# Token mixing of a fused retention and MLP kernel: one 2x2 block product with seven quarter products for eight, and the first loads issued on two queues

## The chip, the cores and the metric

The kernel runs on one core of one Trainium2 chip. The metric is the device time of one execution in microseconds (us), the median over runs. TensorE is called PE here, VectorE DVE, ScalarE ACT, GpSimd POOL, and SyncE SP.

## The reference

Inputs are float32, with batch B = 2, H = 8 heads, S = 768 tokens, head size D = 64, model size DM = 512 and inner size DFF = 1024. Three layers follow each other:

```python
# 1 retention, per head, gamma of the head
state = gamma * state + k[t] v[t]^T ;  y[t] = q[t] state / sqrt(D)
# 2 channel mixing (x is y, x_prev the token before)
xk, xr = mu_k*x + (1-mu_k)*x_prev, mu_r*x + (1-mu_r)*x_prev
x = sigmoid(xr @ w_r) * (relu(xk @ w_k)**2 @ w_v)
# 3 gated MLP with token mixing
h = gelu_tanh(x @ w_in) ;  u, v = h[..., :512], h[..., 512:]
v_n = (v - mean(v)) / sqrt(var(v) + 1e-6) * g_ln
v_s = einsum('ts,bsd->btd', w_sg, v_n) + b_sg[None, :, None]
return x + (u * v_s) @ w_out
```

The change concerns the line of `v_s`, a product of a 768x768 matrix with a 768x512 matrix for each of two batches, and what stands behind it.

## The kernel before

Every dense product is computed as three passes over pairs of rounded halves: an operand is split into a high part (a cast to fp32r) and a low part (the rest), and `passes` (L333) lists high x high, high x low, low x high. `dense` (L319) issues the matmuls of one output tile in three thirds, one for each pass, each a step of its own. `split` (L314) makes the parts: a cast on ACT or DVE and a subtraction on DVE.

The order of all work is made by a planner, the class `Plan`. Each step names its engine, a cost, and the buffers that it reads, writes and needs anew; `Plan.order` (L88) plays the steps through with these costs and writes down the order, which is then each engine's queue, executed strictly in order. A step for "DVE ACT" goes to whichever is free first. SP issues loads and stores, "ADD" stands for accumulating transfers that POOL issues. Buffers come from pools with fixed numbers of slots (`slots`, L208): `p4` (18 of 128 x 2 x 512 words), `t` (13 of 128 x 512), `raw` (3 landing buffers), `ps` (the 8 banks into which PE writes), and single slots aA, aB, bA, bB and cA for split weights.

The program in order: retention in chunks of 128 tokens (`loads` L353, `scores`, `decay`, `state`, `inter`, `intra`, `tokens`), twelve (batch, chunk) pairs, whose `qk` and `kv` tiles of 512 KB are all issued by SP; ten matmuls of zeros (`warm_mm`, L392) run while the first load is under way. Channel mixing follows: `k_tile` (L564), `r_tile` (L568), and the product with `w_v`, in which two blocks of 256 tokens already go by seven quarter products (L580 to L732), with weight sums that accumulating transfers make (`sum_weights`, L603).

Layer 3 works on three blocks of 256 tokens, n = 0, 1, 2. For each n and batch, `c1` (L799) computes the v half, token on partition, with its normalisation on DVE, and splits it into the tiles `vh`; `wsg` (L866) loads and splits one sixth of `w_sg`; `c2` (L854) computes the u half. `c3(g, m)` (L875) is token mixing: for g = 0 and 1 it makes the first 512 tokens of batch g and 128 features in 18 matmuls of 512 columns; for g = 2 the last 256 tokens of both batches in 2 x 18 matmuls of 256 columns. Behind each tile, DVE multiplies by the gain and adds the bias (L888), multiplies by u (L896) and splits the result `gt`. `c4(g)` (L901) multiplies by `w_out`, 12 matmuls of 512 columns for each of 4 m, adds x on DVE (L910) and stores. The calls stand in L917 to L934:

```python
for g in range(B):
    for m in range(KD):
        c3(g, m)
c4(0)
for m in range(KD):
    c3(B, m)
for g in range(1, B + 1):
    c4(g)
```

Of the kernel before, what the change touches and what calls it, by code (L numbers as in the profile page):

```python
# [35 lines left out]
WARM_UP = 10  # L36
EARLY = 5
# [3 lines left out]
T_SLOTS = 13  # L41
# [17 lines left out]
class Plan:  # L59
# [28 lines left out]
    def order(self):  # L88
# [16 lines left out]
        engines = ("PE", "DVE", "ACT", "POOL", "SP", "ADD")  # L105
        idle = {e: BEGIN for e in engines}
        queue = {e: [] for e in engines}
        seq, events, link = [], [(BEGIN, -1, e) for e in engines], 0.0
        started = [False] * n
# [30 lines left out]
        def start(i, t, eng):  # L140
            nonlocal link
# [13 lines left out]
            if eng in ("SP", "ADD"):  # L155
                busy = t + (ISSUE if eng == "SP" else ADD_ISSUE)
                late = link > t + DMA_LEAD + 1.0
                link = max(t + DMA_LEAD, link) + cost / DMA_RATE
                done = link + (DMA_TAIL if late else 0.8)
            else:  # L160
                busy = done = t + cost
# [43 lines left out]
def fused_kernel(ctx, tc, qk, kv, w_k, w_v, w_r, w_in, w_sg, w_out, consts, ydec, b_sg, out):  # L205
# [4 lines left out]
                        "t": {"rs": EARLY, "vs": 2, "cv": 2, "mix": 2, "rk": 2, "vt": 6, "t2": 4, "u": 6, "g": 2, "o": 2}},  # L210
# [142 lines left out]
    def loads(i, what):  # L353
# [38 lines left out]
    def warm_mm():  # L392
        for _ in range(WARM_UP):
            pe.matmul(out=T["warmps"], lhsT=T["warm"][:, :128], rhs=T["warm"], start=True, stop=True)
# [4 lines left out]
    plan.op("PE", 4.0, warm_mm, r=[("warm", 0)], w=[("warmps", 0)], new=[new_b("warm", "warmps")])  # L399
    loads(0, "q")  # L400
    plan.op("SP", .11, const, w=[("con", 0)])
# [110 lines left out]
    for c in range(NCH):  # L512
# [286 lines left out]
    def c1(n, b):  # L799
# [5 lines left out]
        for e in range(2):  # L805
# [6 lines left out]
                    r=[(ps, 0)], w=[(v, e)], new=[new("raw", "raw", v, (128, 2, DM))] if e == 0 else [])  # L812
# [20 lines left out]
        for e in range(2):  # L833
            o = ("vh", b, 2 * n + e)
# [3 lines left out]
            split(lambda e=e: T[v][:, e], o, 0, lambda o=o: T[o][:, 0], lambda o=o: T[o][:, 1], [(v, e)],  # L838
                  [new_p("vh", o)])
# [3 lines left out]
    def u_homes(n):  # L843
        if n == 0:
            return [(new_t("u", ("u", n, m)), ("u", n, m), lambda m=m: T["u", n, m]) for m in range(KD)]
        if n == 1:
            b = ("u", n, "p")
            return ([(new_t("u", ("u", n, m)), ("u", n, m), lambda m=m: T["u", n, m]) for m in range(2)] +
# [166 lines left out]
```

## Time and profile before

| | us |
|---|---|
| median of 3 runs | 357.09 (356.94 to 358.16) |
| the profiled execution's own time | 359.38 |
| its span, first to last instruction | 357.6 |
| PE busy in it | 347.6, 97% |
| DVE busy | 255.8, 72% |
| ACT busy | 159.7, 45% |
| POOL busy | 28.8, 8% |

The span of the profiled execution is the base of the sums; the 1.8 us between it and the execution's own time lie outside of the instructions. The rows that follow below the change are whole lines of the profile's page and of answers of the trace. In the groups, "xcount | busy, mean ns of one | idle before" follows the shapes; in the chain and the timeline, the start and the length come first.

### The profile page before, as it was taken

Reading aid. Unit: us, or ns where it says so; the run is one execution under the profiler, and the core shown is the slowest. Engines: PE = TensorE matmul, PEld = TensorE weight load, DVE = VectorE, ACT = ScalarE, POOL = GpSimd, SP = SyncE. Lnnn points to the kernel's source line nnn. Section 1 sums busy time; section 2 is a strip of 40 time slices with the busy share of each in tenths; the row PEclk is TensorE's granted clock in tenths of the full one; section 3 lists DMA queues with packets and bytes.
Section 4 is the critical chain, followed back from the end, with each engine's and each line's share of the span. In section 5 each row is a group of like instructions: output and inputs, shape, how many; then the busy total and the mean of one; then the engine's idle time right before and its main releaser. Section 6 shows DMA issues by size and latency. Waiting matters only on the chain.

```text
span 357.6 us, 5412 instructions
## 1 busy us (share of the span) xinstructions
PE 347.6 (97%) x2130; PEld 289.7 (81%) x2130; DVE 255.8 (72%) x501; ACT 159.7 (45%) x274; POOL 28.8 (8%) x29
## 2 busy tenths in 40 slices
PE   7988999999999999999999999999999999999995
PEld 4777788888888888888888888888888888899884
DVE  1778999898992664568699998999995656535431
ACT  1044669888972543345589659734542000000000
POOL 0453400000002122101100000000000000000000
PEclk9999999999999999999999999999999999999999
DMA  7999555135544669406354245121130000110122
GB/s 252 415 408 409 210 185 170 59 92 161 158 141 98 106 183 168 73 3 173 66 172 119 60 122 173 44 79 55 45 88 2 0 0 0 60 59 2 58 90 89
DMA packets 15689, 43.32 MB, mean 121 GB/s; under 512 B 1456, under 2 KB 3632, under 8 KB 15664
## 3 DMA queue, kind: packets, MB, share of 16 engines
q1 hardware_dynamic: 12944, 37.73, 30.9%
q0 software_dynamic: 2720, 5.24, 8.6%
q8 instruction: 17, 0.28, 0.3%
q14 instruction: 8, 0.07, 0.1%
HBM read 32.48 MB, written 3.15 MB: 100 GB/s over the span
## 4 chain that ended last, share of the span: by engine, by line
PE 88%; DMA 7%; DVE 3%; issue 1%; SPq 0%; ACT 0%; DVEq 0%; ACTq 0%
PE vp L327 26%; PE kp L327 18%; PE sp L327 14%; PE up L327 9%; PE rp L327 9%; PE op L327 7%; DMA chunk<-qk 3%; DMA chunk<-kv 2%; DMA out<-o 2%; PE y L489 2%; PE sc L416 1%; PE y L478 1%; DVE o L910 1%; DVE xo L316 1%; PE st L452 1%
## 5 line engine op out<-in xcount | busy, mean ns | idle before, releaser
L327 PE MATMUL kp<-xo,wk 128*128 128x512 f32 x288 | 66.2, 390 | 0.0
L327 PEld LDWEIGHTS kp<-xo,wk 128*128 128x128 f32 x288 | 53.9, 188 | 11.5 <-issue 0.3
L327 PE MATMUL sp<-wsg,vh 128*128 128x512 f32 (+1 forms) x288 | 50.2, 336 | 0.0
L327 PEld LDWEIGHTS sp<-wsg,vh 128*128 128x128 f32 x288 | 44.4, 190 | 5.7
L327 PE MATMUL vp<-k,wv 128*128 128x512 f32 x168 | 38.9, 389 | 0.0
L327 PEld LDWEIGHTS vp<-k,wv 128*128 128x128 f32 x168 | 31.5, 188 | 6.5
L327 PE MATMUL vp<-win,x2o 128*128 128x512 f32 x144 | 33.3, 389 | 0.0
L327 PE MATMUL up<-x2o,win 128*128 128x512 f32 x144 | 33.1, 389 | 0.0
L327 PE MATMUL rp<-xo,wr 128*128 128x512 f32 x144 | 33.1, 389 | 0.0
L327 PE MATMUL op<-gt,wout 128*128 128x512 f32 x144 | 33.0, 389 | 0.0
L327 PEld LDWEIGHTS rp<-xo,wr 128*128 128x128 f32 x144 | 27.0, 188 | 5.6
L327 PEld LDWEIGHTS vp<-win,x2o 128*128 128x128 f32 x144 | 27.0, 188 | 5.6
L327 PEld LDWEIGHTS up<-x2o,win 128*128 128x128 f32 x144 | 27.0, 188 | 5.6
L327 PEld LDWEIGHTS op<-gt,wout 128*128 128x128 f32 x144 | 27.0, 188 | 5.6
L888 DVE SCALAR_TENSOR_TENSOR g<-sp,con,bsg 128x512 f32<-128x512 f32 x12 | 9.0, 751 | 21.8 <-PE sp L327 21.8
L316 DVE TENSOR_TENSOR xo<-mix,xo 128x512 fp32r<-128x512 f32 x24 | 17.0, 735 | 8.9 <-ACT xo L249 8.8
L910 DVE TENSOR_TENSOR o<-op,x 128x256 f32<-128x256 f32 (+1 forms) x20 | 8.8, 474 | 19.8 <-PE op L327 13.8
L275 ACT ACTIVATE cv<-raw 128x512 f32<-128x512 f32 x32 | 21.5, 670 | 1.9 <-DMA raw<-w_in 0.7
L327 PE MATMUL vp<-k,ws 128*128 128x512 f32 x96 | 22.1, 389 | 0.0
L612 POOL DMA_DIRECT2D raw<-wv x10 | 12.1, 1211 | 116.9 <-DMA raw<-wv 86.4
L327 PEld LDWEIGHTS vp<-k,ws 128*128 128x128 f32 x96 | 18.0, 188 | 3.7
L290 DVE SCALAR_TENSOR_TENSOR cv<-cv,raw 128x512 int32<-128x512 int32 x28 | 19.8, 714 | 0.6 <-ACT raw L283 0.6
(104 smaller groups left out, 464.5 us busy)
## 6 DMA issues: line engine op xcount, KB each, us to landing
chunk<-qk SPq DMA_DIRECT2D x12, 512.0 KB, 10.1
chunk<-kv SPq DMA_DIRECT2D x12, 512.0 KB, 10.1
raw<-wv POOLq DMA_DIRECT2D x10, 512.0 KB, 5.1
raw<-w_k SPq DMA_DIRECT2D x8, 512.0 KB, 5.3
raw<-w_v SPq DMA_DIRECT2D x8, 512.0 KB, 3.6
raw<-w_in SPq DMA_DIRECT2D x8, 512.0 KB, 3.5
out<-o SPq DMA_DIRECT2D x12, 256.0 KB, 2.2
raw<-w_sg SPq DMA_DIRECT2D x6, 384.0 KB, 3.2
```

The lines of the kernel that those rows point to most:

```text
L275: plan.op("ACT", .68, lambda: act.activation(out=xf(), in_=word(1).bitcast(F32), func=ACTF.Prelu, scale=-F64_REBIAS * F64_SIGN, alpha=1.0 ...
L290: dve.scalar_tensor_tensor(out=xi(), in0=xi(), scalar=3, in1=word(0), op0=ALU.logical_shift_left, op1=ALU.bitwise_or)
L316: plan.op("DVE", .69, lambda: dve.tensor_tensor(out=lo(), in0=src(), in1=hi(), op=ALU.subtract), r=[*keep, (buf, ("hi", part))], w=[(buf, ...
L327: pe.matmul(out=T[ps][:, cols], lhsT=l(), rhs=r(), start=first and q == 0 and i == 0, stop=q == 2 and i == len(grp) - 1, skip_group_check= ...
L416: pe.matmul(out=T["sc", i, p][:, j * CH:(j + 1) * CH], lhsT=a[par[p], 1, j], rhs=a[par[p], 0, j], start=j == 0, stop=j == KD - 1, skip_gro ...
L452: pe.matmul(out=st[par[p], b, j], lhsT=T["kv", i][:, 0, h], rhs=T["vs", i][:, h], start=c == 0 and b == 0 and j == 0, stop=b == B - 1 and ...
L478: pe.matmul(out=y_at(i, j, p), lhsT=T["sbd", (c - 1) % 2][par[p], b, j], rhs=T["qk", i][par[p], 0, j], start=b == 0 and j < 2, stop=False, ...
L489: pe.matmul(out=y_at(i, j, p), lhsT=T["vs", i][:, 2 * j + p], rhs=T["pr", i % 4][:, p, j], start=c == 0 and b == 0 and j < 2, stop=b == B ...
L612: plan.op("ADD", .53, lambda t=t: pool.dma_start(out=T[raw], in_=block_view(*t), accum_op=ALU.add), r=[(b, ("hi" if not t[2] else "lo", p) ...
L888: dve.scalar_tensor_tensor(out=out_, in0=in_, scalar=T["vec"][:, 2, m:m + 1], in1=t.unsqueeze(1).to_broadcast([128, B, BW]) if last else t ...
L910: plan.op("DVE", .69 if g == B else .42, lambda n=n, ps=ps, o=o, m=m, part=part, of=of: dve.tensor_tensor(out=T[o][:, part], in0=T[ps][:, ...
```

## The change

**Token mixing.** The token axis is cut into halves of 384 output tokens, h = 0 and 1, the sum over tokens into even and odd chunks of 128, and the two batches are the two columns of a 2x2 block product. Seven products of (384 x 384) by (384 x 512 features) stand for eight. Each is 4 m x 9 matmuls of 384 columns, 252 in all, where 144 of 512 and 144 of 256 columns stood. Two of the seven add into the banks of an earlier one (`first=False`). The seven weight blocks are sums of one to four quarters of `w_sg`, made by a plain load and accumulating transfers (`sg_sum`: 7 loads and 7 transfers of POOL, 576 KB each), then split (`sg_split`). DVE makes sums of the normalised values (`g_terms`, and in `g_m4`), splits seven sets of three operands (`g_operand`), and combines the products (`stt` and the steps behind it).

**Around it.** `c4` works on (half, batch), 16 tiles of 12 matmuls of 384 columns where 12 of 512 stood, with stores of 192 KB. The normalised values live in `p4` and not in `raw`, `u` in `p4` and in a spare weight slot, and pool `t` has 12 slots. `out` is laid out with the whole token axis in a row.

**Start.** The first two `kv` loads are issued on ACT's queue, the constants go ahead of the first `qk` load on SP's, and three more matmuls of zeros stand behind the scores of chunk 0. The planner's model of loads has a second link for ACT's queue.

```diff
-T_SLOTS = 13
+T_SLOTS = 12
...
-            plan.op("SP", .525, lambda: sp.dma_start(out=T["kv", i], in_=kv[b, c]), r=hold, w=[(("kv", i), 0)],
+            plan.op("SP" if hold else "AQ", .525, lambda: (sp if hold else act).dma_start(out=T["kv", i], in_=kv[b, c]), r=hold, w=[(("kv", i), 0)],
...
+    plan.op("SP", .11, const, w=[("con", 0)])
     loads(0, "q")
-    plan.op("SP", .11, const, w=[("con", 0)])
...
+                if step is scores and i == 0:
+                    plan.op("PE", .65, lambda: warm_mm(FILL), r=[("warm", 0)], w=[("warmps", 0)],
+                            after=plan.writer[("sc", 0, 0), 0])
...
+    def sg_sum(name, terms):
+        raw = ("raw", name)
+        for i, (h, e) in enumerate(terms):
+            view = w_sg[:, e::2, h * HS:(h + 1) * HS]
+            if i == 0:
+                plan.op("SP", .59, lambda view=view: sp.dma_start(out=T[raw], in_=view), w=[(raw, 0)],
+                        new=[new("raw", "raw", raw, (128, NB, HS))], after=plan.writer[("kv", 1), 0])
+            else:
+                plan.op("ADD", .59, lambda view=view: pool.dma_start(out=T[raw], in_=view, accum_op=ALU.add), w=[(raw, 0)])
...
+    def g_product(kind, ps, m, name, weights, first=True):
+        wb, at = sg_at[weights]
+        dense("sp", ps, .1745, passes([
+            ((("gh", name, n), 0, lambda h, n=n: T["gh", name, n][:, h, m * 128:(m + 1) * 128]),
+             (wb, at, lambda h, n=n: T[wb][h][:, at, n])) for n in range(NB)]), first=first, cols=cut, more=True)
+
+    def stt(out, in0, m, op1, in1, r, w, new=()):
+        plan.op("DVE", .56, lambda: dve.scalar_tensor_tensor(out=out(), in0=in0(), scalar=GAIN(m), in1=in1(),
+                                                            op0=ALU.mult, op1=op1), r=[("con", 0), *r], w=[w], new=new)
...
+    def g_n6():
+        for n in range(NB):
+            g_operand("t2", n, g2_at(n))
+        for m in range(KD):
+            ps, v = ("gb", m), ("gv", m)
+            g_product("gb", ps, m, "t2", "g2")
+            stt(half(v), half(ps), m, ALU.subtract, half(v), [(ps, 0)], (v, 0))
+            buf, part, view = v0(m)
+            plan.op("DVE", .55, lambda m=m, v=v, view=view: dve.tensor_tensor(out=view(), in0=T[v][:, cut], in1=bias(0),
+                                                                              op=ALU.subtract),
+                    r=[(v, 0), ("bsg", 0)], w=[(buf, part)])
+            plan.op("DVE", .55, lambda v=v: dve.tensor_tensor(out=T[v][:, cut], in0=T[v][:, cut], in1=bias(1), op=ALU.add),
+                    r=[("bsg", 0)], w=[(v, 0)])
...
+    g_first()
+    sg_sum("g3", [(0, 0), (1, 0)])
+    for n in range(NB):
+        g_terms(n)
+    g_second()
+    g_n6()
+    g_n5()
+    sg_sum("g4", [(0, 0), (0, 1), (1, 0), (1, 1)])
+    sg_split("g3", "bA", 0)
+    sg_split("g4", "bA", 1)
+    sg("g22", [(1, 1)], "bB", 0)
+    g_n7()
+    g_m3()
+    g_m4()
+    c4(0, 0)
+    for m in range(KD):
+        gt_split(1, 1, m, half(("gw", m)), (("gw", m), 0))
+    c4(0, 1)
+    c4(1, 1)
+    for m in range(KD):
+        gt_split(1, 0, m, half(("gv", m)), (("gv", m), 0))
+    c4(1, 0)
```

The products run in the order `g_first` (b11 x g11), `g_second` (b21 x g12, into the same banks), `g_n6` (t2 x g2), `g_n5` (t1 x g1), `g_n7` (t3 x g3), `g_m3` (b22 x g4, into the banks of n5), `g_m4` (t4 x g22, into the banks of n7), and PE's queue takes the thirds of a tile apart where a low part is late.

On SP's queue at the start of the program (`chunk` are the tiles of qk and kv, `scr<-ydec` the decay table), before:

```order
L357 DMA chunk<-qk 128x1024
L372 DMA con<-consts 128x212
L360 DMA chunk<-kv 128x1024
L357 DMA chunk<-qk 128x1024
L360 DMA chunk<-kv 128x1024
L381 DMA scr_128<-ydec 128x512
```

With the change, on SP and then on ACT:

```order
L379 DMA con<-consts 128x212
L364 DMA chunk<-qk 128x1024 x2
L388 DMA scr_120<-ydec 128x512
```

```order
L367 DMA chunk<-kv 128x1024 x2
L256 ACT_TABLE_LOAD
```

The two `kv` loads have moved from between the `qk` loads to the head of ACT's queue, and the constants to the head of SP's.

On DVE in token mixing, one output tile's steps before (`sp` is what PE wrote, `g` the gated tile, `gt` its split):

```order
L888 SCALAR_TENSOR_TENSOR g<-sp,con,bsg 128x512
L896 TENSOR_TENSOR g<-g,u 128x256 x2
L249 CAST gt_2716<-g 128x512
L316 TENSOR_TENSOR gt_2717<-g,gt_2716 128x512
L888 SCALAR_TENSOR_TENSOR g<-sp,con,bsg 128x512
```

With the change, the stretch behind the last tile of n6 (`vh<-vf` are low parts of operands, `sg` of weight blocks, `gv` and `gw` the running combinations):

```order
L931 SCALAR_TENSOR_TENSOR gv<-sp,con,gv 128x384
L1010 TENSOR_TENSOR spare_2614<-gv,bsg 128x384
L1013 TENSOR_TENSOR gv<-gv,bsg 128x384
L323 TENSOR_TENSOR vh<-vf,vh 128x512 x2
L892 TENSOR_TENSOR sg_2818<-raw,sg_2817 128x1152
L1024 TENSOR_TENSOR gw<-gv,gw 128x384 x4
L892 TENSOR_TENSOR sg_2818<-raw,sg_2817 128x1152
L892 TENSOR_TENSOR sg_2951<-raw,sg_2950 128x1152
L323 TENSOR_TENSOR vh<-vf,vh 128x512 x5
L931 SCALAR_TENSOR_TENSOR gw<-sp,con,gw 128x384
L949 SCALAR_TENSOR_TENSOR gw<-gw,u 128x128
L949 SCALAR_TENSOR_TENSOR gw<-gw,spare_2613 128x256
```

Operand and weight splits, which stood before the mixing, now stand between the steps that empty PE's banks.

On PE where token mixing meets the output product, before:

```order
L327 MATMUL sp<-wsg_2254,vh 128x512 x3
L327 MATMUL sp<-wsg_2496,vh 128x512 x3
L327 MATMUL op<-gt_2716,wout_2163 128x512 x4
L327 MATMUL op<-gt_2717,wout_2163 128x512 x4
L327 MATMUL op<-gt_2716,wout_2164 128x512 x4
```

With the change (`sg_2950` is the high part of g22, the weights of the last product):

```order
L334 MATMUL sp<-sg_2951,vh 128x384 x3
L334 MATMUL sp<-sg_2817,vh 128x384 x12
L334 MATMUL op<-gt_2767,wout_2182 128x384 x4
L334 MATMUL op<-gt_2768,wout_2182 128x384 x4
L334 MATMUL op<-gt_2767,wout_2183 128x384 x4
...
L334 MATMUL sp<-sg_2950,vh 128x384 x12
L334 MATMUL op<-gt_2768,wout_2182 128x384 x4
```

The last third of the last product stands behind 40 matmuls of the first output product.

## Rows read from the trace of the kernel before

**Rows 1.** The page, head, parts 1 and 2.

```profile
span 357.6 us, 5412 instructions
PE 347.6 (97%) x2130; PEld 289.7 (81%) x2130; DVE 255.8 (72%) x501; ACT 159.7 (45%) x274; POOL 28.8 (8%) x29
PEclk9999999999999999999999999999999999999999
```

**Rows 2.** The chain that ended last, in order of time.

```profile
48.55 34.72 PE kp L327 x152
...
270.94 32.64 PE sp L327 x144
303.58 10.88 PE op L327 x48
314.46 17.27 PE sp L327 x144
331.74 13.64 PE op L327 x60
...
353.58 0.67 DVE o L910
```

**Rows 3.** Groups by shape, PE and its weight loads, token mixing.

```profile
L327 PEld LDWEIGHTS sp<-wsg,vh 128*128 128x128 f32 x288 | 44.4, 190 | 5.7
...
L327 PE MATMUL sp<-wsg,vh 128*128 128x512 f32 x144 | 32.8, 389 | 0.0
...
L327 PE MATMUL sp<-wsg,vh 128*128 128x256 f32 x144 | 17.4, 283 | 0.0
```

**Rows 4.** Groups by shape, DVE, layer 3 and the earlier sums.

```profile
L888 DVE SCALAR_TENSOR_TENSOR g<-sp,con,bsg 128x512 f32<-128x512 f32 x12 | 9.0, 751 | 21.8 <-PE sp L327 21.8
...
L316 DVE TENSOR_TENSOR vh<-raw,vh 128x512 fp32r<-128x512 f32 x12 | 7.7, 683 | 0.0
...
L896 DVE TENSOR_TENSOR g<-g,u 128x256 f32<-128x256 f32 x16 | 6.1, 422 | 0.3
...
L316 DVE TENSOR_TENSOR wsg<-raw,wsg 128x768 fp32r<-128x768 f32 x6 | 5.7, 950 | 0.0
...
L623 DVE TENSOR_TENSOR ws<-raw,ws 128x1024 fp32r<-128x1024 f32 x4 | 4.9, 1219 | 0.1
...
L896 DVE TENSOR_TENSOR g<-g,raw 128x512 f32<-128x512 f32 x4 | 2.8, 692 | 0.3
```

**Rows 5.** Busy time by stretch, last piece of c2 and start of mixing.

```profile
260.00:270.90 10.90, 10.90 (x50) 9.03 (x49) 10.21 (x31) 5.40 (x9) 0.00 (x0) 1.00 0.26 72
270.90:280.00 9.10, 9.10 (x42) 7.54 (x41) 3.69 (x8) 0.60 (x1) 0.00 (x0) 1.00 0.01 2
```

The columns are the stretch, its length, busy us (and instructions) of PE, PEld, DVE, ACT and POOL, PE's granted clock, DMA share, and GB/s.

**Rows 6.** Timeline of the start, SP's issues of the two kv loads.

```profile
1.66 0.42 SPq L360 DMA_DIRECT2D chunk<-kv  x1
...
2.60 0.43 SPq L360 DMA_DIRECT2D chunk<-kv  x1
```

**Rows 7.** Busy time by stretch, the first microseconds.

```profile
2.00:3.00 1.00, 1.00 (x4) 0.42 (x3) 0.00 (x0) 0.02 (x1) 0.00 (x0) 1.00 0.81 283
3.00:4.00 1.00, 1.00 (x4) 0.34 (x3) 0.00 (x0) 0.00 (x0) 0.00 (x0) 1.00 0.97 363
...
5.00:6.00 1.00, 1.00 (x6) 0.43 (x6) 0.00 (x0) 0.00 (x0) 0.00 (x0) 1.00 0.96 156
...
8.00:10.00 2.00, 1.42 (x25) 1.12 (x27) 1.56 (x3) 0.00 (x0) 0.00 (x0) 1.00 1.03 416
```

**Rows 8.** Timeline of the retention, PE's longest wait and DVE's behind it.

```profile
27.57 1.09 PE L489 MATMUL y<-prs,vs 128*64 128x128 f32 x16 [1.91 <-issue]
...
28.55 1.29 DVE L503 TENSOR_TENSOR x<-y,scr 128x512 f32<-128x512 f32 x2 [2.60 <-PE y L489]
```

**Rows 9.** Timeline of POOL, two accumulating transfers of the earlier sums.

```profile
138.84 1.19 POOL L612 DMA_DIRECT2D raw<-wv  x1 [1.40 <-DMA raw<-wv]
145.00 1.21 POOL L612 DMA_DIRECT2D raw<-wv  x1 [4.96 <-DMA raw<-wv]
```

More of the change, by code (lines that the diff above doesn't have):

```diff
@@ L104, in order @@
         pending = {}
-        engines = ("PE", "DVE", "ACT", "POOL", "SP", "ADD")
+        engines = ("PE", "DVE", "ACT", "POOL", "SP", "ADD", "AQ")
         idle = {e: BEGIN for e in engines}
@@ L901, in c4 @@
[L901 to L915 removed]
+    HS = S // 2
@@ new lines, in fused_kernel, with sg, value, g_operand @@
+    sg_at = {}
+    def sg(name, terms, tag, at):
+        sg_sum(name, terms)
+        sg_split(name, tag, at)
+    def value(n, b, e):
+        v = ("v", n, b)
+        return v, e, lambda: T[v][:, e]
+    def g_operand(name, n, at):
+        buf, part, view = at
+        o = ("gh", name, n)
+        split(view, o, 0, lambda: T[o][:, 0], lambda: T[o][:, 1], [(buf, part)], [new_p("vh", o)])
+    g2 = [("g2", n) for n in range(NB)]
+    def g2_at(n):
+        return g2[n], 0, lambda: T[g2[n]]
+    def g_terms(n):
+        b11, b12, b22 = value(n, 0, 0), value(n, 1, 0), value(n, 1, 1)
+        combine(b11, b11, b12, ALU.subtract)
+        combine(g2_at(n), b22, b11, ALU.add, [new_t("t2", g2[n])])
+        combine(b12, b22, b12, ALU.subtract)
@@ new lines, in bias, with gt_tag, gating, go @@
+    def bias(h):
+        return T["bsg"][:, h * HS:(h + 1) * HS]
+    def gt_tag(h, b):
+        return {(0, 0): "aA", (0, 1): "bA", (1, 1): "bB", (1, 0): "aA"}[h, b]
+    def gating(h, b, m, src, key, sign):
+        for n in ((0, 1), (1, 2))[h]:
+            lo, hi = max(n * BW, h * HS), min((n + 1) * BW, (h + 1) * HS)
+            _, ub, view = us[n][m]
+            part, of = slice(lo - h * HS, hi - h * HS), slice(b * BW + lo - n * BW, b * BW + hi - n * BW)
+            def go(part=part, of=of, view=view):
+                if sign < 0:
+                    dve.scalar_tensor_tensor(out=src()[:, part], in0=src()[:, part], scalar=-1.0, in1=view()[:, of],
+                                             op0=ALU.mult, op1=ALU.mult)
+                else:
+                    dve.tensor_tensor(out=src()[:, part], in0=src()[:, part], in1=view()[:, of], op=ALU.mult)
+            plan.op("DVE", .42 if hi - lo == BW else .26, go, r=[(ub, m)], w=[key])
@@ new lines, in g_n5 @@
+    def g_n5():
+        for n in range(NB):
+            g_operand("t1", n, value(n, 0, 0))
+        for m in range(KD):
+            ps, v, w = ("gd", m), ("gv", m), ("gw", m)
+            g_product("gd", ps, m, "t1", "g1")
+            plan.op("ACT", .5, lambda m=m, ps=ps, w=w: act.mul(T[w][:, cut], T[ps][:, cut], GAIN(m)), r=[(ps, 0), ("con", 0)],
+                    w=[(w, 0)], new=[new_t("gw", w)])
+            plan.op("DVE", .55, lambda v=v, w=w: dve.tensor_tensor(out=T[w][:, cut], in0=T[v][:, cut], in1=T[w][:, cut],
+                                                                   op=ALU.subtract), r=[(v, 0)], w=[(w, 0)])
@@ L917, in fused_kernel, with g_m4 @@
+    def g_m4():
+        for n in range(NB):
+            b21 = value(n, 0, 1)
+            combine(b21, g2_at(n), b21, ALU.subtract)
+            g_operand("t4", n, b21)
+        for m in range(KD):
+            ps, v = ("ge", m), ("gv", m)
+            g_product("ge", ps, m, "t4", "g22", False)
+            stt(half(v), half(ps), m, ALU.subtract, half(v), [(ps, 0)], (v, 0))
+            gating(1, 0, m, half(v), (v, 0), -1)
     for j in range(4):
```

184 lines of the change are left out of this document (104 added, 80 removed).

## The prediction

> **What bounds the kernel now.** Read the page first [rows 1]: PE is busy 97% of the span and its granted clock is 9 or more tenths of full speed in every slice, so nothing is to be won from the clock. The chain of waits in order of time [rows 2] says where the rest lies. From 48.55 us on it is PE without a gap, through token mixing (32.64 and 17.27 us) and the output products (10.88, and 13.64 and the rest behind it), and only the start belongs to loads and other engines. Here a matmul saved is time saved, as long as the other engines keep up. The price of a matmul is its pitch, and that comes from the chain, not from the groups: 32.64 / 144 = 226.7 ns for 512 columns, 17.27 / 144 = 119.9 ns for 256. The groups show 389 and 283 ns for the same matmuls [rows 3], because pipelined matmuls overlap; that mean is a latency. DVE is the engine to watch: 72% overall, but 10.21 of 10.90 us in the stretch before mixing, then 3.69 of 9.10 us [rows 5]. Mixing is where DVE has had room, and the change spends that room.
>
> **The change part by part.**
>
> PE, mixing. It removes 32.64 + 17.27 = 49.91 us [rows 2]. It adds 252 matmuls of 384 columns, a width that this trace does not have; its neighbours bound it, 119.9 and 226.7 ns. The two lie on a line of 13 ns plus 0.417 ns a column, so I take the middle, 173.3 ns, and 252 x 173.3 = 43.7 us. A weight load's row says 190 ns [rows 3], which would be a floor above 173 if loads could not overlap; at 256 columns PE goes on at 119.9 ns with the same load, so they do. Mixing: -6.2 us.
>
> PE, output. 192 matmuls of 384 columns at 173.3 ns are 33.3 us. Before it was 144 of 512 at 226.7 ns, 32.6 us. The columns are the same, 48 more starts cost +0.6 us. PE together: -5.6 us, all on the path, +-0.5 for the pitch.
>
> DVE in mixing. From the end of the second product (when the step behind its last tile may start) to the last third of the last product, both queues can be added up. PE has 168 matmuls of products and 40 of the first output product ahead of that third: 208 x 173.3 ns = 36.05 us. DVE has 64 instructions that must be done by then: 13 scalar_tensor_tensor of 384 columns out of PE's banks, 17 tensor_tensor of 384, 13 of 512 (splits), 9 of 256, 9 of 128, and 3 weight splits of 1152. Prices [rows 4]: 692 at 512 and 422 at 256 columns give 1.055 ns a column, so 556 ns at 384 and 287 at 128. The scalar_tensor_tensor on a bank with the gain takes 751 at 512, so 616 at 384. Splits take 683. From 950 at 768 and 1219 at 1024 I get 1353 at 1152. Sum: 8.0 + 9.5 + 8.9 + 3.8 + 2.6 + 4.1 = 36.8 us, plus some 0.2 us until DVE sees PE's last column. So DVE is late by 36.95 - 36.05 = 0.9 us, and PE waits for it, in one piece or at several thirds. If neighbours overlap a little it is 0; if each instruction costs 0.04 us more, it is 3. I take +0.9 us. Note that the edit's own cost for the bank step, 0.56, is below the row's 0.616, so the planner's order has no room for this.
>
> DVE before and behind that stretch. Before the mixing, 12 value splits of 0.683 and 6 of `w_sg` (0.950) leave the c1 and c2 stages; 4 weight splits of 1.353 and some operand splits come in. Less is asked of an engine that kept up. The sums of values (9 x 0.69 = 6.2 us) are due only when the first two products are over, 72 x 173.3 ns = 12.5 us into mixing. Behind the stretch, DVE has about 22 us of work (32 pieces of the output sum, 9 splits, 12 bank steps and gatings) beside 152 matmuls, 26.3 us. Hidden, with little to spare.
>
> ACT takes the casts of the gated tiles from DVE, and 8 bank copies; its queue has been empty in mixing (0.60 of 9.10 us [rows 5]). Hidden.
>
> Weight sums. 7 loads of 576 KB replace 6 of 384 KB, and 7 accumulating transfers are new, while the DMA engines are used to 26% and 1% [rows 5]. The nearest row for a transfer is the earlier sums: from one issue to the next that waits for it, 145.00 - 138.84 = 6.2 us [rows 9]. The longest sum, g4, has four transfers, up to 25 us. Its landing buffer is free when the split of g2 is done, which ACT's and DVE's queues hold ahead of the last c1 and c2 pieces, 2 x 10.9 us of PE before mixing, and its own split is wanted some 26 us into mixing: 25 us in about 48. A transfer would have to take over 11 us to be late. POOL has nothing queued behind them. Cost 0; if the cover went, ACT would stand at the cast of a sum with gelu steps behind it, and PE would run out of banks.
>
> The start. The kv loads are issued on ACT at the head of the program in place of 1.66 and 2.60 us on SP [rows 6]. Then later loads are issued up to 0.9 us sooner. But the DMA engines' share is 0.81 in the third microsecond, 0.97 in the fourth and 0.96 in the sixth, although they move only 283, 363 and 156 GB/s there against 416 later [rows 7]. They are occupied, just slow, so a second queue has little to fill. The same bytes must land before chunk 5 in either order. From the idle fifth of the third microsecond and a part of the slow stretch I take -0.3 us, and bounds of -1.4 (all bytes of 2 to 7 us at 410 GB/s) and +0.5 (the constants ahead of the first load: one issue of 0.4 us). The three extra matmuls fill a wait. [...]
>
> The order elsewhere. The retention's queues are reshuffled by the planner, with one slot less in `t`. PE's order from the first kp tile to the last up tile is nearly the same, and what hides the rest is PE's gapless row. I add 0, and a look at PE's idle time there. The tail behind the last matmul (the sum, the store) keeps its shape: 0.
>
> **Sum.** -5.6 + 0.9 - 0.3 = -5.0 us on the span of 357.6. The profiled execution's own time, 359.38, is 2.3 us above the median of the runs; a difference carries over: 357.09 - 5.0 = 352.1 us.
>
> **The rivals.**
>
> A, the start gives more. PE's longest wait in the retention, 1.91 us, is on no data, and DVE waits 2.60 us behind it [rows 8]; from there to 48.55 us DVE is the engine that everything waits for. Six more instructions on PE ahead of it and other load times may move or remove this wait. That would give up to -1.9 more: 350.2. Against it: the same number of loads saturates the engines then.
>
> B, the saving is eaten partly. Each DVE instruction waits a little for semaphores, and the thirds of n6, n5 and n7 that wait for low parts each stop PE too; 2 to 4 us late in all instead of 0.9 gives 353.2 to 355.2.
>
> C, DVE becomes the bound and the kernel is slower. The place is the same stretch. At 0.9 us of lateness the gain is 5.0; it is gone when DVE is late by 5.9 us, that is, when each of its 64 instructions costs 0.08 us more than its row. With 0.12 us more, about 360. For it: most of these steps are chains on one tile. Against it: in before such a chain, 0.751 + 2 x 0.422 + cast and split, follows PE with time left over. [...]
>
> **How the numbers follow.** My forecast has 0.60 and its own range is 350.6 to 353.6. A has 0.17, B 0.15, C 0.05, and 0.03 is left for PE losing time in the earlier stages. A measurement of this kernel can tell about 0.5%, 1.8 us, from no change. Faster by over that, below 355.3: the forecast, A, and most of B, less a little for what I have not seen, 0.87. Within it 0.08, slower 0.05. The range that should hold the time 8 times in 10 is 349.3 to 355.2: it takes in A with the pitch a little lower, and B to its end.
>
> **What would show it.** Right: matmul groups of 252 and 192 at a pitch near 173 ns in the chain, mixing and output together 77 us plus what PE waits; PE idle some 1 us in the products, released by DVE's splits or bank steps; the first kp run starting near 48.3 us; accumulating transfers done before their casts. Wrong: a pitch away from 173, PE waits of several us in mixing with DVE at 100%, ACT waiting for a weight sum, or a kp run that starts 2 us off.

## The result, and the profile after

The change takes 353.45 us (median of 4 runs, 352.29 to 353.73) against 357.01 us of the kernel before (4 runs): a ratio of 0.9893, 95% interval 0.9874 to 0.9912, 3.6 us less. That is within the range of 349.3 to 355.2 us and 1.35 us above the forecast of 352.1. The sum behind the forecast, however, contains one term with the wrong sign, the start, and two smaller terms that erred the other way made up for part of it.

The head of the page and its first part, for the kernel after:

```profile
span 351.8 us, 5577 instructions
PE 345.2 (98%) x2145; PEld 296.5 (84%) x2145; DVE 277.4 (79%) x561; ACT 178.5 (51%) x306; POOL 37.6 (11%) x36
```

The profiled execution's own time is 353.52 us, as good as the median. The chain of waits, in order of time (start, length, engine, tile, line):

```profile
48.57 34.68 PE kp L334 x152
...
270.92 41.90 PE sp L334 x240
312.83 6.93 PE op L334 x40
319.76 2.08 PE sp L334 x12
321.84 26.36 PE op L334 x152
```

Against [rows 2]: the first kp run starts at 48.57 where it started at 48.55, mixing at 270.92 where it started at 270.94. Token mixing takes 41.90 + 2.08 = 43.98 us where it took 49.91; the output products take 33.29 us where they took 32.7. So mixing paid, as forecast, and the start gave nothing against this execution. The groups by shape, for PE and its weight loads in mixing (count, busy time, mean ns, idle time before):

```profile
L334 PE MATMUL sp<-sg,vh 128*128 128x384 f32 x252 | 44.3, 335 | 0.0
L334 PEld LDWEIGHTS sp<-sg,vh 128*128 128x128 f32 x252 | 43.7, 188 | 0.4 <-ACT vh L256 0.2
```

No idle time stands before the products of mixing. In the stretch for which the prediction added up DVE's queue, from the end of the second product (283.4) to the last third of the last one (319.8), the busy times are these (stretch, its length, then busy us of PE, PEld, DVE, ACT, POOL, granted clock, DMA share, GB/s):

```profile
283.40:319.80 36.40, 36.40 (x211) 36.10 (x210) 34.66 (x69) 14.15 (x24) 0.00 (x0) 1.00 0.00 1
```

PE fills it, and DVE fills 95% of it. The last weight sums' transfers are issued 6.5 and 6.7 us apart (POOL's timeline) and land in good time. ACT waits for a sum once for long, 5.46 us up to 247.1, ahead of mixing. The prediction had named such a wait as a sign of being wrong; here it cost nothing, for PE has no wait from 260 us to the end:

```profile
255.81 1.17 POOL L882 DMA_DIRECT2D raw<-w_sg  x1 [10.10 <-DMA raw<-w_sg]
262.32 1.16 POOL L882 DMA_DIRECT2D raw<-w_sg  x1 [5.34 <-DMA raw<-w_sg]
269.02 1.16 POOL L882 DMA_DIRECT2D raw<-w_sg  x1 [5.55 <-DMA raw<-w_sg]
```

The start is where the forecast and the profile part. PE's first pieces (in brackets the idle time before a piece and what ended it), and behind it the heads of SP's and of ACT's timeline:

```profile
1.20 4.45 PE L401 MATMUL warm<-warm 128*128 128x512 bf16 x10 [1.20 <-DVE x L505]
7.43 2.08 PE L423 MATMUL sc<-chunk 64*128 64x128 f32 x16 [1.79 <-DMA chunk<-qk]
9.44 1.46 PE L401 MATMUL warm<-warm 128*128 128x512 bf16 x3
10.83 1.12 PE L459 MATMUL st<-vs,chunk 128*64 128x64 f32 x16
11.74 1.92 PE L496 MATMUL y<-prs,vs 128*64 128x128 f32 x16
```

```profile
0.74 0.39 SPq L379 DMA_DIRECT2D con<-consts  x1
1.19 0.89 SPq L364 DMA_DIRECT2D chunk<-qk  x2
```

```profile
0.74 0.89 ACTq L367 DMA_DIRECT2D chunk<-kv  x2
```

PE waits 1.79 us for the first qk tile and starts the scores at 7.43 us; then each piece takes 1.6 to 1.8 times what the same piece takes later (the scores 1.16 us, the state product 0.69). From there to the first kp run PE's list of waits holds nothing more. The chain runs over PE from the scores to 25.6 us, so what PE does in the first chunk is on it; from there to 47.4 us it runs over DVE. In the second profile of the same kernel, below, it runs over the late first load and the loads behind it up to 36.1 us instead, and then over DVE: several engines are nearly balanced here, and not every microsecond won at the head arrives at the kp run.

### The profile page after: what moved, and what is told of

Same layout as the page of the kernel before. It is cut to its first block, busy times and chain, and to the rows that moved or that the text cites. A ratio compares the mean times of both kernels' runs of the same rounds, so it can differ in the third digit from the quotient of the medians.

```text
span 351.8 us, 5577 instructions
## 1 busy us (share of the span) xinstructions
PE 345.2 (98%) x2145; PEld 296.5 (84%) x2145; DVE 277.4 (79%) x561; ACT 178.5 (51%) x306; POOL 37.6 (11%) x36
## 4 chain that ended last, share of the span: by engine, by line
PE 91%; DVE 6%; DMA 2%; issue 0%; SPq 0%; DVEq 0%
PE vp L334 26%; PE kp L334 18%; PE sp L334 13%; PE op L334 9%; PE up L334 9%; PE rp L334 9%; DVE prs L432 2%; PE sc L423 2%; DMA chunk<-qk 2%; PE y L496 2%; DVE x L510 1%; DVE cv L297 1%; PE st L459 1%; DVE mix L543 1%; DVE xo L323 1%; PE y L485 1%
## 5 line engine op out<-in xcount | busy, mean ns | idle before, releaser
L334 PE MATMUL sp<-sg,vh 128*128 128x384 f32 x252 | 44.3, 335 | 0.0
L334 PEld LDWEIGHTS sp<-sg,vh 128*128 128x128 f32 x252 | 43.7, 188 | 0.4 <-ACT vh L256 0.2
L334 PE MATMUL vp<-k,wv 128*128 128x512 f32 x168 | 38.9, 389 | 0.0
L334 PE MATMUL op<-gt,wout 128*128 128x384 f32 x192 | 33.6, 334 | 0.0
L334 PEld LDWEIGHTS op<-gt,wout 128*128 128x128 f32 x192 | 33.3, 188 | 0.0
L334 PE MATMUL vp<-win,x2o 128*128 128x512 f32 x144 | 33.3, 389 | 0.0
L432 DVE TENSOR_TENSOR prs<-sc,con 128x512 f32<-128x512 f32 x24 | 15.3, 681 | 9.7 <-PE sc L423 9.6
L975 DVE TENSOR_TENSOR o<-op,x 128x256 f32<-128x256 f32 (+1 forms) x32 | 9.7, 352 | 11.2 <-PE op L334 11.1
L297 DVE SCALAR_TENSOR_TENSOR cv<-cv,raw 128x512 int32<-128x512 int32 x24 | 17.7, 746 | 0.3 <-ACT raw L290 0.3
```

What stands on the lines that cost most here:

```text
L297: dve.scalar_tensor_tensor(out=xi(), in0=xi(), scalar=3, in1=word(0), op0=ALU.logical_shift_left, op1=ALU.bitwise_or)
L334: pe.matmul(out=T[ps][:, cols], lhsT=l(), rhs=r(), start=first and q == 0 and i == 0, stop=q == 2 and i == len(grp) - 1, skip_group_check= ...
L432: plan.op("DVE", .66, lambda p=p: dve.tensor_tensor(out=T["pr", i % 4][:, p], in0=heads(T["sc", i, p]), in1=T["mask"].unsqueeze(1).to_broa ...
L975: dve.tensor_tensor(out=T[o][:, part], in0=T[ps][:, part], in1=T["x2", n][:, m, of], op=ALU.add),
```

## The experiments

**Two controls.** The kernel before and the changed kernel were run again, unchanged, since one profiled execution stood for each.

> The kernel before, unchanged, profiled and timed once more. Theory P (the profiled execution of before was a long one: its own time, 359.4, is 2.3 above the median of its runs, and the 1.91 us wait of PE on no data in the retention is what made it long): this profile has a span near 355.2, the kp run starts near 46.5 us instead of 48.55, and everything behind is as it was. Theory Q (the wait belongs to the kernel): the kp run starts at 48.5 again, with a PE wait of 1.5 to 2 us before the y group, and the 2.3 us lie elsewhere. Ratio to the kernel before: 1.000 in either case.

Measured: 357.63 us (12 runs), ratio 1.0004 [0.9983, 1.0025]. This execution has a span of 355.1 us, 2.5 less than the first; its own time is 356.88. Mixing starts at 268.45 us, and PE's longest waits between 5 and 48 us are these (total, times, longest; the other two are 0.2 us each):

```profile
PE sc L416 <- DMA chunk<-qk: 1.9, 2, 1.4
PE st L452 <- DVE vs L434: 1.6, 1, 1.6
```

The wait of 1.91 us on no data [rows 8] is not among them. So the first profile of before had an execution that lost 2.5 us in the retention, and the better base for the change is a kp run at 46.07 us, not 48.55: the median span of these 12 runs is 355.4 us.

> The changed kernel, unchanged, for a tighter ratio and the spread of its profile. Theory P: about 3.6 us under before (ratio 0.990), kp run starting at 48.5 again. Theory Q: the gap of the two profiles, 5.8 us (ratio 0.984).

Measured: 353.20 us, ratio 0.9867 [0.9843, 0.9892], span 351.7, kp run at 48.54, mixing 41.89 + 2.08. The changed kernel's start is the same in both its profiles: 48.57 and 48.54 us. It loses 2.5 us against the second profile of before, or some 2 us by the medians, since that profile lies 0.3 us under the median span of its runs and this one 0.4 us above.

**The change taken apart.** First the change with its start undone:

```diff
-SHARED = 7.5
+SHARED = 0.0
...
-            plan.op("SP" if hold else "AQ", .525, lambda: (sp if hold else act).dma_start(out=T["kv", i], ...
+            plan.op("SP", .525, lambda: sp.dma_start(out=T["kv", i], ...
...
-    plan.op("SP", .11, const, w=[("con", 0)])
     loads(0, "q")
+    plan.op("SP", .11, const, w=[("con", 0)])
...
-                if step is scores and i == 0:
-                    plan.op("PE", .65, lambda: warm_mm(FILL), ...
```

> The changed kernel with its start undone: all first loads on SP's queue in the old order, no matmuls of zeros behind the first scores. Token mixing and the output product are those of the change. If the new start is worth what the two profiles say (0.0 us: 48.57 against 48.55), this takes as long as the change, within 0.5 us. Theory P: the old start is usually about 2 us shorter than the new one, so this is near 351.4, 5.6 us under before and 2 us under the change, with the kp run starting near 46.5.

Measured: 351.12 us, ratio 0.9827 [0.9801, 0.9853]. From its chain:

```profile
46.15 34.72 PE kp L334 x152
...
268.55 41.89 PE sp L334 x240
...
317.37 2.08 PE sp L334 x12
...
```

And the new start alone, put into the kernel before (the same edits the other way round):

> The kernel before with the new start alone: two kv loads on ACT's queue, the constants ahead of the first qk load, three more matmuls of zeros. Theory P: about 2 us slower than before (ratio 1.005), kp run at 48.5. If the start is worth nothing either way: ratio 1.000. My forecast for this part was 0.3 us faster (ratio 0.999).

Measured: 359.52 us, ratio 1.0044 [1.0027, 1.006]; kp run at 48.70 us. So the start costs some 2 us by the medians, alone (359.52 against 357.47) as in the change (353.20 against 351.12); by the ratios it is 1.6 and 1.4. Mixing alone is worth 6 us.

**Which part of the start.** Each of the next four keeps the queues of PE, DVE and POOL as they were in the kernel that it is derived from, but for the lines shown. The first two are derived from the mixing-only kernel. The two first kv loads on ACT, with no change of the order:

```diff
-            plan.op("SP", .525, lambda: sp.dma_start(out=T["kv", i], in_=kv[b, c]), ...
+            plan.op("SP", .525, lambda: (sp if hold else act).dma_start(out=T["kv", i], in_=kv[b, c]), ...
```

> The mixing-only kernel with one edit: the two first kv loads are issued on ACT instead of SP. The order of the instructions on PE, DVE and POOL stays as in the mixing-only kernel, the constants stay behind the first qk load, no matmuls of zeros are added. Theory L (the first qk load shares the DMA engines with the kv loads and lands late): the first scores start near 7 us instead of 5 us, the first kp run starts 1.5 to 2.4 us later than the 46.15 us of the mixing-only kernel, and the time is 352.6 to 353.5 us, against 351.1. Theory O (the loads are harmless; the planner's new order of the retention costs the 2 us): the kp run starts near 46.2 us and the time is 351.1 +- 0.5 us.

Measured: 351.58 us, ratio 0.9823 [0.98, 0.9846]; first scores at 5.32 us, kp run at 46.32. Theory L's price falls, its mechanism does not. The first qk load, issued at 0.74 us together with the first kv load, lands 4.5 us later, where with all loads on SP it lands 3.4 us after its issue (list of issues, number, size, us to landing; the mixing-only kernel, then this one):

```profile
chunk<-qk SPq DMA_DIRECT2D x1, 512.0 KB, 3.4
chunk<-qk SPq DMA_DIRECT2D x1, 512.0 KB, 4.5
```

So the second queue alone makes it 1.1 us later, but the ten matmuls of zeros run until 5.1 us and hide all but 0.2 us of it.

The constants first, all on SP:

```diff
-    loads(0, "q")
     plan.op("SP", .11, const, w=[("con", 0)])
+    loads(0, "q")
```

> The mixing-only kernel with one edit: the constants are loaded ahead of the first qk load, all on SP; the order on PE, DVE, ACT and POOL stays. Theory L: the first load lands later by one issue and the constants' bytes, 0.2 to 0.7 us, and the kp run by as much or less (46.2 to 46.9 us); time 351.1 to 351.8 us. Theory O: no change, 351.1 +- 0.5 us. A result of 352.5 or more would say that the constants' place, not the second queue, is the late load's cause.

Measured: 350.83 us, ratio 0.9813 [0.9783, 0.9843]; first scores at 5.57 us, directly behind the zeros; the first load lands 3.4 us after its issue at 1.19 us. So this is harmless as well. (The kp run of the profiled execution, at 47.86, stands behind a wait of 1.91 us on no data, the one of [rows 8] again.)

The next two are derived from the changed kernel. Without the three matmuls of zeros:

```diff
-                if step is scores and i == 0:
-                    plan.op("PE", .65, lambda: warm_mm(FILL), r=[("warm", 0)], w=[("warmps", 0)], ...
```

> The changed kernel without the three matmuls of zeros behind the first scores; every other instruction keeps its engine and place. Theory L: they stand in a wait, so nothing moves: kp run at 48.5 us, time 353.3 +- 0.5 us. Theory F (they stand in the way: 1.46 us of PE ahead of the first state product): kp run at 47.2 to 48.0 us, time 352 to 352.8 us. Theory K (what the start loses is the clock that PE has after its idle stretch from 5.6 to 7.4 us): the clock stays at the lower level for longer, kp run 48.6 to 49.5 us, time 353.4 to 354.3 us.

Measured: 352.82 us, ratio 0.9858 [0.9832, 0.9884], and the kp run at 47.24 us. In the trace theory F is right: the run starts 1.33 us sooner, nearly all of the 1.46 us that the zeros took. But this execution, 352.19 us, is the fastest of the four by 0.5 us, and the medians do not show it clearly, 0.4 us with intervals that overlap.

And with 14 zeros at the head of the program, so that PE is at work until the first tile has nearly landed:

```diff
-WARM_UP = 10
+WARM_UP = 14
```

> The changed kernel with 14 instead of 10 matmuls of zeros at the head of the program, so that PE works until about the moment at which the first qk load lands (7.4 us); every other instruction keeps its engine and place. Theory K (the late start costs because PE idles from 5.6 to 7.4 us and then runs the first chunk at the lower clock level, where the scores take 2.08 us instead of 1.16): the first chunk runs at the higher level, the first kp run starts 0.8 to 2.4 us sooner than 48.57 us, time 350.9 to 352.4 us. Theory L (the late load alone sets the start, whatever the clock): kp run at 48.4 to 48.7 us, time 353.2 +- 0.5 us.

Measured: 351.15 us, ratio 0.981 [0.9779, 0.9841], kp run at 47.33 us. The first pieces of PE's timeline:

```profile
1.19 5.86 PE L401 MATMUL warm<-warm 128*128 128x512 bf16 x14 [1.19 <-DVE x L505]
7.85 1.16 PE L423 MATMUL sc<-chunk 64*128 64x128 f32 x16 [0.80 <-DMA chunk<-qk]
8.95 0.82 PE L401 MATMUL warm<-warm 128*128 128x512 bf16 x3
9.70 0.69 PE L459 MATMUL st<-vs,chunk 128*64 128x64 f32 x16
10.21 1.26 PE L496 MATMUL y<-prs,vs 128*64 128x128 f32 x16
```

Four more matmuls that compute nothing, and the median is 2 us lower, although the scores start 0.4 us later than in the profile after. The four runs lie in two pairs, 350.1 and 352.2 us; the profile is of the slowest, 352.27, and what the faster pair gains is in no trace. In the profile the same four pieces take 3.9 us where they took 6.6, and 1.2 us arrive at the kp run. Theory K is right in part: the low clock costs at least these 1.2 us, and the rest of the 2.5 us, the late load and the zeros, was not separated further. The granted clock itself is seen in the second profile of the changed kernel (windows, columns as above):

```profile
5.26:8.00 2.74, 0.00 (x1) 0.00 (x0) 0.87 (x2) 0.00 (x0) 0.00 (x0) 1.00 1.03 423
8.00:11.00 3.00, 2.99 (x19) 1.97 (x19) 0.97 (x2) 0.00 (x0) 0.77 (x1) 0.53 1.04 416
...
12.00:14.00 2.00, 2.00 (x36) 1.71 (x33) 0.00 (x0) 0.00 (x0) 1.81 (x2) 1.00 1.03 412
```

PE idles for 2.74 us, then works at 0.53 of its full clock for 3 us, and is back at 1.00 from 12 us on. (The profile after shows 1.00 throughout in that column, with durations as long: 2.08 us for the scores and 1.46 for the three zeros, against 1.98 and 1.46 here. That its clock was low as well is inferred from them.)

**The cause, and the mend.** Neither part of the loads' new order was slow alone, so the suspicion fell on the pair. The runs from here on stand on another chip, where before took 357.51 us; the ratios carry the comparison. Here the constants go back behind the first qk load, and nothing else of the changed kernel moves on any engine:

```diff
     def loads(i, what):
...
-            plan.op("SP", .525, lambda: sp.dma_start(out=T["qk", i], in_=qk[b, c]), ...
+            plan.op("SP", .525, lambda: (sp.dma_start(out=T["qk", i], in_=qk[b, c]), i == 0 and const()), ...
...
-    plan.op("SP", .11, const, w=[("con", 0)])
+    plan.op("SP", .11, lambda: None, w=[("con", 0)])
```

> The changed kernel with one edit: the constants are issued behind the first qk load instead of ahead of it; the kv loads stay on ACT, the zeros stay, every instruction of PE, DVE, ACT and POOL keeps its place. Theory J (the loss needs both parts of the start at once: the first qk load is issued 0.45 us behind the two kv loads because SP issues the constants first, and then shares the DMA engines with them): the load lands near 5.3 us instead of 7.4 to 8.0, PE's zeros run until about then, the first scores take 1.16 us instead of 2.08, the first kp run starts at 45.0 to 46.4 us, time 349.9 to 351.4 us. Theory O (the planner's order or the zeros cost the 2 us): kp run at 47.5 us or later, time over 352.3 us.

Measured: 349.19 us (349.12 to 349.31), ratio 0.975 [0.9728, 0.9773]: 4 us faster than the change, and a little under the lower end of what theory J expected. The first load's landing in the profile after and here, SP's first issues here, PE's first pieces, and the kp run in the chain:

```profile
chunk<-qk SPq DMA_DIRECT2D x1, 512.0 KB, 6.2
chunk<-qk SPq DMA_DIRECT2D x1, 512.0 KB, 4.6
```

```profile
0.74 0.39 SPq L364 DMA_DIRECT2D chunk<-qk  x1
1.19 0.42 SPq L379 DMA_DIRECT2D con<-consts  x1
```

```profile
1.19 4.45 PE L401 MATMUL warm<-warm 128*128 128x512 bf16 x10 [1.19 <-DVE x L505]
5.57 1.78 PE L423 MATMUL sc<-chunk 64*128 64x128 f32 x16
7.29 0.82 PE L401 MATMUL warm<-warm 128*128 128x512 bf16 x3
8.04 0.69 PE L459 MATMUL st<-vs,chunk 128*64 128x64 f32 x16
```

```profile
44.17 34.69 PE kp L334 x152
```

One issue of 0.39 us, moved behind another, takes 4.4 us off the start. The load is there when the zeros end, PE does not idle, and by the durations the clock rises during the first scores: these take 1.78 us, not the 1.16 that theory J expected, and the three zeros behind them 0.82, as long as in the run with longer zeros. (The column of the granted clock has 1.00 here too, from 3 us on.) It is the best version of this study.

The expectation has the first load, in the change, issued behind both kv loads. The timelines show it 0.45 us behind the first and at the same time as the second, 1.19 us. By the 4.6 us that it takes beside a second queue it would land at some 5.8 us (an estimate, 1.19 + 4.6); it lands at 7.4. Something more goes with the pair: the DMA engines' third microsecond, in the profile after and in this one (windows, columns as above), reads:

```profile
2.00:3.00 1.00, 1.00 (x4) 0.42 (x3) 0.00 (x0) 0.94 (x1) 0.00 (x0) 1.00 0.45 96
2.00:3.00 1.00, 1.00 (x4) 0.43 (x3) 0.00 (x0) 0.95 (x1) 0.00 (x0) 1.00 0.83 303
```

All five profiles with the pair move 48 to 96 GB/s there, and the nine others 235 to 324. Between these two rows lie 207 KB, half a microsecond at the later 410 GB/s (an estimate), so this is not all of it either. Why the two together slow the engines is not shown.

Then the loads as before, in the planner's new order and without the zeros:

> The changed kernel with its first loads issued as before (first qk, constants, kv, all on SP) and without the zeros; the order of DVE, ACT and POOL and the rest of PE's order stay those of the change. Theory J: the order itself is neutral, kp run at 45.5 to 46.6 us, time 350.5 to 351.6 us. Theory O: kp run at 47.5 us or later, time over 352.3 us.

Measured: 351.02 us, ratio 0.9804 [0.9771, 0.9837], kp run at 45.76 us. The new order by itself is neutral, or better by a few tenths of a us that the runs' spread (350.05 to 352.39) hides; theory O falls. Queue and order pay only together: with the second queue and the old order the time was 351.58, with the new order and the old queue 351.02, with both 349.28 (the next run, also without the zeros). In the old order PE's longest wait is then 2.0 us for a later qk tile, and in the new one 0.7; that the new order can use the earlier kv tiles is my reading of it.

And the kernel with the constants put back, without the three zeros as well:

> The kernel of the run on the constants' place, without the three matmuls of zeros as well: it may be the best of all. If PE is still what the start waits for, the zeros' 0.8 us come off: kp run at 44.5 to 45.6 us, time 349.3 to 350.6 us. If DVE or the loads set the start by then, the zeros only fill a wait: kp run and time as with them, within 0.4 us.

Measured: 349.28 us, ratio 0.9753 [0.973, 0.9776], kp run at 44.67. The same: with the load in time, the zeros do fill a wait (here PE waits 0.7 us for a qk tile and 0.3 us for DVE in their place).

**DVE's room in mixing, and rival C.** In the mixing-only kernel each bank step of the products, from the second product on, gets one more DVE instruction:

```diff
-        plan.op("DVE", .56, lambda: dve.scalar_tensor_tensor(out=out(), in0=in0(), scalar=GAIN(m), in1=in1(),
-                                                            op0=ALU.mult, op1=op1), r=[("con", 0), *r], w=[w], new=new)
+        def go():
+            dve.scalar_tensor_tensor(out=out(), in0=in0(), scalar=GAIN(m), in1=in1(), op0=ALU.mult, op1=op1)
+            dve.tensor_tensor(out=out(), in0=out(), in1=out(), op=ALU.max)
+        plan.op("DVE", .56, go, r=[("con", 0), *r], w=[w], new=new)
```

> The mixing-only kernel with one more DVE instruction behind every scalar_tensor_tensor on a bank of the products from the second on (maximum of the tile with itself, 384 columns, the result unchanged): 20 instructions, 16 or 17 of which stand ahead of the last product's last third or feed it, 13 of them in the stretch of my sum. It doubles as the test of rival C. Sum of the prediction (DVE and PE have nearly equal work in that stretch): 13 x 0.556 = 7.2 us more of DVE, less 0.5 to 1.5 us of slack, so the products end 5.5 to 7.5 us later, time 356.5 to 359 us against 351.1: more than before's gain over again nearly gone. Rival (DVE has room: its instructions overlap with each other and with waits): products at most 2 us longer, time under 353.5 us.

Measured: 360.12 us, ratio 1.0057 [1.0029, 1.0084], 9 us more than without (8.2 by the ratios, the two runs standing on two chips), 0.6% slower than the kernel before. That is a little over the 356.5 to 359 us that were expected. The profiled execution, 362.22, is the slowest of the seven and has the wait of [rows 8] again, ahead of the stretch looked at. The products, from their first matmul at 271.0 us to their last at 330.55 and without the 40 output matmuls between them, take 52.6 us against 43.97, 8.6 us more. 16 of the 20 additions stand ahead of the last product's last third, not only the 13 that the expectation priced: 16 x 0.557 = 8.9 us. PE's waits, and a look at the middle of the stretch (windows, columns as above):

```profile
PE sp L334 <- DVE vh L323: 3.6, 5, 1.4
...
PE sp L334 <- DVE gw L929: 0.9, 2, 0.5
```

```profile
298.00:300.00 2.00, 0.50 (x2) 0.25 (x2) 1.97 (x5) 0.62 (x1) 0.00 (x0) 1.00 0.00 0
300.00:304.00 4.00, 4.00 (x16) 4.00 (x17) 3.39 (x6) 3.02 (x5) 0.00 (x0) 0.63 0.01 4
304.00:310.00 6.00, 6.00 (x35) 6.00 (x34) 5.39 (x7) 2.47 (x5) 0.00 (x0) 0.96 0.00 0
```

The first thing to see is that PE now waits where the prediction said, at the low parts that DVE makes (`vh`), and DVE is busy in 1.97 of 2.00 us there. The second was not expected: behind PE's idle stretch from 297.9 to 299.3 us the granted clock falls, to 0.50 in 302 to 304 us, and 49 matmuls take 10.37 us, 211.6 ns each in place of 173.3. That is up to 1.9 of the 8.6 us. Here a DVE that is late costs PE twice.

## Why the prediction was right, and where it was not

Against the second execution of before, the one without the odd wait, the spans give each term of the sum (355.1 to 351.8):

| term | predicted, us | measured, us |
|---|---|---|
| PE, mixing and output | -5.6 | -5.6 (43.7 and 33.3 at the pitch) |
| DVE's lateness | +0.9 | +0.3 |
| the start | -0.3 | +2.5 (mixing starts at 270.92, not 268.45) |
| the tail | 0 | -0.5 |
| sum | -5.0 | -3.3 |

**PE: right.** 240 matmuls in 41.90 us are 174.6 ns each, 12 in 2.08 are 173.3, and 152 in 26.36 are 173.4. The line through the neighbours' widths held at a width that the trace did not have. The weight load of 188 ns did not set a floor. The groups' mean of 335 ns is again a latency.

**DVE: the durations right, the sum too high.** Bank steps took 612 ns against my 616, 128-column pieces 283 to 292 against 287, weight splits 1353 against 1353; two of the groups in the stretch:

```profile
L931 DVE SCALAR_TENSOR_TENSOR spare<-sp,con,spare 128x384 f32<-128x384 f32 x4 | 2.4, 612 | 0.0
L892 DVE TENSOR_TENSOR sg<-raw,sg 128x1152 fp32r<-128x1152 f32 x3 | 4.0, 1353 | 0.0
```

The groups list 69 instructions in the stretch, the 64 of the sum and 5 others. Count times mean, they add up to 38.9 us, and the 64 to 36.8 as predicted, but the stretch shows 34.66 us of DVE busy. The record of an instruction overlaps that of the next, by 0.06 us on average; the timeline of DVE just ahead of the last third:

```profile
315.14 0.42 DVE L952 TENSOR_TENSOR spare<-spare,u 128x256 f32<-128x256 f32 x1
315.48 0.55 DVE L959 TENSOR_TENSOR gt<-spare,gt 128x384 fp32r<-128x384 f32 x1
315.95 0.28 DVE L952 TENSOR_TENSOR spare<-spare,u 128x128 f32<-128x128 f32 x1
316.15 0.61 DVE L931 SCALAR_TENSOR_TENSOR spare<-sp,con,spare 128x384 f32<-128x384 f32 x1
316.80 0.43 DVE L952 TENSOR_TENSOR spare<-spare,u 128x256 f32<-128x256 f32 x1
...
317.81 0.69 DVE L323 TENSOR_TENSOR vh<-vf,vh 128x512 fp32r<-128x512 f32 x1
```

315.14 + 0.42 is 315.56, and the next one, on another tile, starts at 315.48; where the next one needs the result, as the gating at 316.80 needs the bank step of 316.15 (0.61 us), it starts 0.04 us behind its end. The prediction had named this case ("if neighbours overlap a little it is 0") and not taken it. The last low part is done at 318.50, and PE wants it at 319.76: 1.3 us of slack, where I had 0.9 us of lateness. The idle time of PE that was named as a sign of being right, some 1 us in the products, did not come. The 0.2 us until DVE sees PE's last column was an estimate of mine that no run shows as a term; in the profiles before and after, the last sum on DVE starts 0.03 us behind the end of PE's last matmul (353.53 and 353.56; 348.20 and 348.23).

**The start: wrong, and this is the step that failed.** The prediction priced the second queue from the first microseconds' rates, and the constants "ahead of the first load: one issue of 0.4 us" as a bound of +0.5. Both were looked at alone. Together they let one load of 512 KB on ACT's queue go ahead of the one load that PE waits for, and another go with it: it is issued at 1.19 us, the kv loads at 0.74 and 1.19, and it lands at 7.4 to 8.0 us, where it landed at 4.1 before and at 5.3 with the second queue alone. The runs with one part each (351.58 and 350.83 us against 351.12) and the run with the constants put back (349.19) show the pair as the cause; how the two slow the DMA engines at once stays open. The statement that "the three extra matmuls fill a wait" was wrong in the change: with no wait behind the first scores left, they took 1.46 us of the path; in the run with the load in time they cost nothing. And the page's row of granted clock, from which I took that nothing was to be won there, said nothing of a PE that is made to idle.

The second queue itself did more than I gave it. In the fifth to seventh microsecond the DMA engines moved 316, 205 and 344 GB/s in the second execution of before, and 357, 386 and 427 in the run with the constants put back; with nothing else changed, the second queue took the kernel from 351.02 to 349.28 us. Beside the second queue the first load lands 4.5 us after its issue and without it 3.4 (the kv loads on ACT, and mixing only). But the slow stretch of [rows 7], which the run with the new order and the old queue has as well (209, 176 and 385 GB/s in the same three microseconds), is gone with a second queue: what I took from those rows, that such a queue has little to fill, did not hold.

**The tail: a small miss.** I had said that it keeps its shape. Before, the last sum of 512 columns took 0.69 us; now two pieces of 256 and 128 columns follow the last matmul, 0.62 us together, and the store is smaller. From PE's last matmul to the end of the span it is 3.6 us (348.20 to 351.8) in place of 4.1 (353.53 to 357.6).

**The base: a sign that came by luck.** The forecast subtracts its sum from the median of the runs, so the long first execution is not in it. It is in the sign that the prediction named: a first kp run "near 48.3 us" would be right, one 2 us off wrong. The run came at 48.57, and that is luck: the first execution of before had lost 2.5 us in the retention by something of its own, and the change loses as much by its start. Against the next execution the sign says wrong, 48.57 where 46.07 less 0.3 was due. The forecast itself lies within 1.35 us for a like reason: the start is 2.8 us worse than its term, and DVE and the tail are 1.1 us better than theirs; the rest is that the medians differ by 3.56 us and these two spans by 3.3.

**The rivals.** A said that the 1.91 us on no data might vanish. It is absent from both profiles of the change, but also from the second profile of before, and it came back in two runs with the old order (constants first, more DVE); it is in 3 of 6 profiles with the old order of the retention and in none of 8 with the new one. That is too few to credit the order with it. B, PE stopped by late thirds, did not occur: mixing lost 0.3 us in all. C did not occur, but its mechanism and point are shown: with 8.9 us more of DVE ahead of the last third the kernel is slower than before. Of these 8.9 us some 2 found room on DVE if all of the 1.9 us are the clock's, and less if not.

**What the change is worth.** Mixing by seven products for eight: 6 us (351.12 against 357.47). The second queue, with the first load kept first and the planner's order for it: 2 us more (349.19). The change as it was made gets some 4 of these 8.

## What to carry to other kernels

Before a second queue is used at the start of a program, ask which load the first engine waits for, and issue that load ahead of, or at least together with, the first load on every queue: the kv bytes that were moved ahead of the awaited ones here cost some 2 us (353.20 us against 351.12 without the new start). Where two engines are nearly balanced, add up pitches, not durations, on the vector engine too (here durations of 38.9 us stood in 34.66 us of busy time), and remember that a TensorE that has idled may come back at about half its clock, as it did behind 2.74 us here (0.53 for 3 us), so that a wait costs more than its length. Take two profiles of the kernel before as a base whenever the effect that you look for is about one per cent.

## What the runs showed of the hardware

- The clock behind an idle stretch differs. It was at the lower level, 0.50 to 0.53, behind 2.74 us (second profile of the change), 2.04 us (the kv loads on ACT, at 31 us) and 1.42 us (more DVE, at 299 us); durations of the lower level (2.08 us for the scores, 1.16 later) followed 1.79 us in the profile after, though the column has 1.00 there. By their durations the zeros ahead of that wait had all run at the lower level themselves: 4.45 us for ten, where three took 1.46 us in the second profile of the change, at a granted 0.50 for most of it, and 0.82 in the run with longer zeros, at 1.00. It stayed at 1.00 behind the 1.91 us of [rows 8], and behind 2.26 us in the mixing-only kernel (at 8.4 us). What decides between them is open.
- A first load of 512 KB landed 3.2 to 3.4 us after its issue when all loads were on SP; 4.5 to 4.6 us when ACT issued another at the same time and one 0.45 us later; 6.2 to 6.8 us when SP issued the constants first and ACT's first load was 0.45 us ahead. In the last case the DMA engines moved 48 to 96 GB/s in the third microsecond, and 235 to 324 otherwise.
- Three of the 14 profiled executions have a wait of 1.9 us of PE in the retention, before a product of `y`, that nothing in the profile explains. Its cause was not tried.
